# Forty scratch writes issued by GpSimd's queue instead of SyncE's, in a kernel of local attention and a long convolution

## The chip, the cores and the metric

The kernel runs on one core of a Trainium2 chip. The core has five engines with instruction queues of their own: TensorE (PE in the profile), VectorE (DVE), ScalarE (ACT), GpSimd (POOL) and SyncE (SP). DMAs are issued by instructions in these queues and carried out by 16 DMA engines that all queues share. The metric is the time of one execution on the device, in microseconds (us). Before the change it is 208.29 us, the median of three runs (208.14, 208.29, 210.05).

## What is computed

Two independent parts, whose results stand side by side in the output (2048 rows, 576 + 576 columns, bf16):

```python
def _A_ref(x, wqkv, wo):            # x: 1 x 2048 x 576
    q, k, v = ...                   # x @ wqkv, 32 heads of 18
    idx = pos[:, None] - off[None, :]            # off = 0, 2, 4, ..., 14
    logits = einsum("bhsd,bhswd->bhsw", q, k[idx]) * scale     # masked where idx < 0
    o = einsum("bhsw,bhswd->bhsd", softmax(logits), v[idx])
    return o @ wo
def _B_ref(q, k, v, shift_k, ssm_k, ssm_D):      # all 2048 x 576
    kv = causal_conv4(k, shift_k) * v            # four taps along the rows
    y = irfft(rfft(kv, 4096) * rfft(ssm_k, 4096))[:2048]       # per column
    return q * (y + kv * ssm_D)
```

Part A is attention over eight earlier rows at a step of two. Part B is a convolution of 2048 rows with a kernel of the same length, in each of 576 columns.

## The kernel before

All inputs fit into SBUF, the on-chip memory, in stages. The order of the work is written out by hand: the string ORDER (lines 18 to 46) lists some 500 steps, and lines 667 to 672 call them one by one. Each engine executes its own instructions in the order in which these calls emit them, and a DMA stands in the queue of the engine that issues it. Waits between engines, and between a DMA and the users of its data, are put in automatically where two instructions touch the same part of a buffer or of a scratch tensor. An engine that waits holds everything behind it in its queue.

Part B multiplies in the frequency domain. A transform of length 4096 (the 2048 rows, padded) is made in two levels. For the first level the rows are taken as 128 x 16; a step transforms two of the 16 columns of rows (`c2` from 0 to 7), for all 576 channels, with one 128 x 128 table each for the real and the imaginary part. There are sixteen such steps: x0 to x7 for the data (`sx`, x_part, line 470) and k0 to k7 for the long kernel (`kp`, k_part, line 479). ORDER has them as x0, x1, x2, x3, k0, k1, x4, x5, k2, x6, x7, k7, k3, k4, k6, k5, with steps of part A between. All of them go through s1_part (line 426): three chunks (`ch` 0 to 2) of 384 columns, each two matmuls (L432) into PSUM and one eviction (L436) by ACT into a staging buffer; L436 calls evac, whose ScalarE instruction is L103 in the profile. After the third chunk the staging buffer is written to scratch in DRAM, Dx or Dk, in two DMAs of 288 KB (L439), one for each half of the channels. Scratch is needed since the second level reads the same numbers with partitions and rows exchanged: in Dx and Dk, 128 partitions each write four rows of 288 elements (576 bytes).

The staging buffers form a ring of two, `vsr` (line 193). So the evictions of a step can begin only when both writes of the step two before have landed.

The second level (k_spec, x_spec, from L541) loads Dk and Dx (L547), evicts spectra by ACT, multiplies them on DVE (g_prod, L563), and transforms back (g_inv, L576). Its results go to scratch Dy by DMAs of 576 KB that GpSimd issues (L581), and are read again for the last level (L637, y_step), multiplied by q and written out.

The long kernel comes with its rows and columns exchanged. It is loaded by 16 transposing DMAs (load_knat, L262) into `kst`, a ring of seven slots, and written out as rows to the scratch tensor Kt in eight DMAs of 288 KB (k_rows, L265, steps `kw`). From Kt, k_tr (L477) loads two columns of rows for each k step. The memory of `kst` is used later for the products of attention (l_mul, L487 and L491).

The convolution of four taps (kv_conv, L455 to L468) runs on DVE ahead of the x steps. Part A is spread over the same time: projections on PE (L377, L384), eight products of q with shifted k on DVE (L487, L491) summed over the head on PE (L504), softmax, products with v (p_mul, L588), sums (L599) and the output projection (L610).

SyncE's queue holds nearly all DMAs: loads, transposes (L262, and L414 and L424 for tables), the writes of L265 and L439, loads from scratch (L477, L547, L637) and the writes of the output. GpSimd's queue holds a few memsets and index patterns at the start, then one memset (L389, which clears the left edge of V), three small DMAs that copy edge columns of V between partitions (v_halo, L393, 96 partitions x 6 x 16 elements), and the eight Dy writes.

Of the kernel before, what the change touches and what calls it, by code (L numbers as in the profile page):

```python
# [49 lines left out]
def kernel(  # L50
# [13 lines left out]
    nc = tc.nc  # L64
# [33 lines left out]
    def psb():  # L98
        return psum("b", 2, 512)

    def evac(dst, src, scale=None, on="s"):
        if (how["ev"] or on) == "s":
            nc.scalar.activation(dst, src, ACT.Copy, **({} if scale is None else {"scale": scale}))  # L103
        elif scale is None:
            nc.vector.tensor_copy(dst, src)
        else:
            nc.vector.tensor_scalar(dst, src, scale, None, op0=ALU.mult)

    Kt = dram.tile([S, D], BF16, name="Kt")
# [5 lines left out]
    def by_f1(Dd, dh, r0, n):  # L115
        return Dd[dh].rearrange("r f d -> f r d")[:, r0:r0 + n, :]
# [82 lines left out]
    kst = Ring(*[r2.take(2, D) for _ in range(7)])  # L199
# [62 lines left out]
        nc.sync.dma_start_transpose(st[:, b % 2:b % 2 + 1, :], B_ssm_k[:, 128 * b:128 * b + 128])  # L262

    def k_rows(g):
        nc.sync.dma_start(Kt[256 * g:256 * g + 256, :].rearrange("(b p) d -> p b d", p=128), kst[g])  # L265
        kst.drop(g)

    def load_D():
# [157 lines left out]
    def s1_part(src, key, c2, ch, Dd, add_d):  # L426
        sf = src.rearrange("p t d -> p (t d)")
        vst = vsr.get((key, c2)) if ch == 0 else vsr[(key, c2)]
        ps = psb()
        for ri in range(2):  # L430
            extra = add_d and c2 == 0 and ri == 0 and ch < 2
            nc.tensor.matmul(ps[:, ri, 0:384], T1[:, ri, :], sf[:, 384 * ch:384 * ch + 384], start=True, stop=not extra)  # L432
            if extra:
                n = 384 if ch == 0 else 192
                nc.tensor.matmul(ps[:, ri, 0:n], row0[0:1, :], Db[0:1, 384 * ch:384 * ch + n], start=False, stop=True)
        evac(vst[:, :, 384 * ch:384 * ch + 384], ps[:, :, 0:384])  # L436
        if ch == 2:
            for dh, (d0, d1) in enumerate(DCH):
                nc.sync.dma_start(by_f1(Dd, dh, 4 * c2, 4), vst.rearrange("p r (t d) -> p (r t) d", t=2)[:, :, d0:d1])  # L439
            vsr.drop((key, c2))  # L440

    def wqt_step():
# [27 lines left out]
    def x_part(c2, ch):  # L470
        c = c2 // 2
        s1_part(tAr[c][:, 2 * (c2 % 2):2 * (c2 % 2) + 2, :], "x", c2, ch, Dx, False)
        if c2 % 2 and ch == 2:
            tAr.drop(c)
# [4 lines left out]
    def k_part(c2, ch):  # L479
        s1_part(ktr[c2], "k", c2, ch, Dk, True)  # L480
        if ch == 2:
            ktr.drop(c2)
# [160 lines left out]
    def y_step(i, u):  # L643
# [11 lines left out]
        if u:  # L655
# [4 lines left out]

    STEP = dict(tj=t_junk, wm=warm, t0=t_ident, t1=t_pad, tv=t_padv, t2=t_first, t3=t_second, tw=t_w2, t4=t_heads, t5=t_mask,
                lwq=load_wq, wt=wqt_step, lx=load_x, xt=x_tr, ia=ia_table, im=ia_minus, ib=ib_table, kw=k_rows, lwt=load_wqt, ld=load_D, sk=sk_step, qk=qk_step, qt=qk_tail_step, lk=load_k, lv=load_v, lwv=load_wv,
                lkn=load_knat, lwo=load_wo, cv=kv_conv, sx=x_part, kt=k_tr, kp=k_part, v=v_step, vz=v_zero, vh=v_halo, lm=l_mul, lb=l_sum,
                sm=softmax, kl=lambda i: w_load(Dk, "k", i), xl=lambda i: w_load(Dx, "x", i),
# [38 lines left out]
```

## Time and profile before

| | us |
|---|---|
| median of three runs | 208.29 |
| the profiled execution, as timed | 211.04 |
| its span, first to last instruction | 209.1 |
| PE busy | 185.2 |
| DVE busy | 177.8 |
| ACT busy | 160.7 |
| POOL busy | 12.9 |

The profile is of one execution. Busy times count instructions that compute; a DMA is seen by its issue on an engine's queue (SPq is SyncE's queue, POOL GpSimd's), by its landing, and by its packets. q1 in the profile is the DMA queue that SyncE feeds, q0 the one that GpSimd feeds. The granted TensorE clock was 0.999 of full speed. From the list of DMA issues (number, size of one, median us from issue to landing):

| transfer | issued by | number | KB | us to landing |
|---|---|---|---|---|
| Dx written | SP | 16 | 288 | 4.2 |
| Dk written | SP | 16 | 288 | 4.4 |
| Kt written | SP | 8 | 288 | 3.6 |
| Dx loaded | SP | 8 | 576 | 5.9 |
| Dk loaded | SP | 8 | 576 | 6.8 |
| Dy written | POOL | 8 | 576 | 6.2 |
| V's edge columns | POOL | 3 | 18 | 7.6 |

The Kt writes are issued from 34.0 to 51.4 us, the Dx writes from 41.6 to 86.2 and the Dk writes from 62.8 to 106.3.

### The profile page before, as it was taken

The numbers are of one execution on the slowest core, as the hardware profiler recorded it, in microseconds if no ns is written. First come the engines' busy times: TensorE is split into PE (matmuls) and PEld (weight loads), VectorE is DVE, ScalarE is ACT, GpSimd is POOL, SyncE is SP. The second block draws the span as 40 slices with busy tenths as digits, with TensorE's granted clock in tenths as the row PEclk, the third lists the DMA queues.
The fourth block names the chain that finished last, engine by engine and source line by source line (L and its number), as shares of the span: only waits on it lengthen the run. The fifth ranks groups of instructions, "written<-read, shape, count | busy, mean of one in ns | idle before, by whom it ended". The sixth has DMA issues, their size and how long they took to land.

```text
span 209.1 us, 6223 instructions
## 1 busy us (share of the span) xinstructions
PE 185.2 (89%) x2645; PEld 118.3 (57%) x2645; DVE 177.8 (85%) x157; ACT 160.7 (77%) x244; POOL 12.9 (6%) x39
## 2 busy tenths in 40 slices
PE   0899999999989797999789888799999999989890
PEld 0655454444435564554367665566766778766680
DVE  6529999999899999899798989989999979954452
ACT  3669876989777896989799999899999982515421
POOL 8300000000000000001000201110102011000000
PEclk9999999999999999999999999999999999999999
DMA  5999999999997979899997998999799599899894
GB/s 162 317 316 396 239 211 158 311 198 299 275 368 247 260 181 261 241 214 367 261 250 226 264 242 240 310 350 246 256 390 246 179 330 377 248 335 304 223 314 135
DMA packets 66797, 56.20 MB, mean 269 GB/s; under 512 B 16673, under 2 KB 60306, under 8 KB 66770
## 3 DMA queue, kind: packets, MB, share of 16 engines
q1 hardware_dynamic: 65520, 51.04, 91.9%
q0 software_dynamic: 1248, 4.77, 5.9%
q8 instruction: 20, 0.33, 0.7%
q14 instruction: 7, 0.06, 0.1%
q10 hardware_dynamic: 2, 0.00, 0.0%
HBM read 31.04 MB, written 21.23 MB: 250 GB/s over the span
## 4 chain that ended last, share of the span: by engine, by line
PE 46%; ACT 27%; DMA 16%; issue 6%; DVE 2%; SPq 0%; ACTq 0%; DVEq 0%
ACT area L103 24%; PE psB L377 8%; PE psA L377 5%; DMA Dx<-area 5%; PE psA L610 5%; DMA out_dram<-area 4%; DMA Dy<-area 4%; PE psA L384 3%; PE psA L576 3%; PE psB L599 3%; PE psB L432 2%; DMA Dk<-area 2%; PE psA L599 2%; PE psA L432 2%; DMA area<-in_B_shift_k_dram 2%
## 5 line engine op out<-in xcount | busy, mean ns | idle before, releaser
L103 ACT ACTIVATE area<-psA 128x576 bf16<-128x576 f32 (+7 forms) x117 | 83.5, 757 | 33.1 <-PE psB L610 15.0
L103 ACT ACTIVATE area<-psB 128x576 bf16<-128x576 f32 (+5 forms) x113 | 80.2, 757 | 7.9 <-PE psB L377 4.0
L588 DVE TENSOR_TENSOR area<-area,area 128x4096 bf16<-128x4096 bf16 x18 | 40.6, 2284 | 0.9 <-DMA area<-area 0.8
L487 DVE TENSOR_TENSOR area<-area 128x4096 bf16<-128x4096 bf16 x16 | 35.8, 2286 | 1.0 <-PE psA L504 0.7
L377 PEld LDWEIGHTS <-area 128*128 128x128 bf16 x160 | 15.5, 98 | 17.5
L377 PE MATMUL psB<-area,area 128*128 128x512 bf16 x100 | 23.1, 379 | 0.0
L563 DVE TENSOR_TENSOR area<-area 128x2304 bf16<-128x2304 bf16 x16 | 21.1, 1351 | 1.3 <-ACT area L103 1.0
L461 DVE TENSOR_TENSOR area<-area,area 128x2304 bf16<-128x2304 bf16 x16 | 21.0, 1348 | 0.0
L541 PEld LDWEIGHTS <-W 128*64 128x64 bf16 x256 | 14.0, 108 | 12.3 <-issue 11.1
L610 PE MATMUL psA<-area,area 32*128 32x288 bf16 x288 | 18.7, 281 | 1.6 <-ACT area L103 1.1
L610 PE MATMUL psB<-area,area 32*128 32x288 bf16 x288 | 18.7, 281 | 0.0
L384 PEld LDWEIGHTS <-area 128*32 128x32 bf16 x360 | 15.2, 142 | 5.6 <-issue 2.8
L599 PEld LDWEIGHTS <-ident 64*64 64x64 bf16 x576 | 15.3, 106 | 5.1 <-issue 3.5
L610 PEld LDWEIGHTS <-area 32*128 32x128 bf16 x576 | 15.5, 93 | 4.6 <-issue 2.2
L384 PE MATMUL psA<-area,area 128*32 128x512 bf16 x280 | 16.7, 384 | 0.4 <-ACT area L103 0.2
L432 PEld LDWEIGHTS <-T 128*128 128x128 bf16 x96 | 8.6, 97 | 14.6 <-issue 9.3
L541 PE MATMUL psB<-area,W 128*64 128x288 bf16 x152 | 14.7, 290 | 1.8 <-ACT area L103 1.1
L455 DVE TENSOR_TENSOR area<-area,area 128x2304 bf16<-128x2304 bf16 x12 | 15.8, 1350 | 0.1
L576 PEld LDWEIGHTS <-IAt 64*128 64x128 bf16 x256 | 12.4, 94 | 5.8 <-issue 1.5
L432 PE MATMUL psB<-area,T 128*128 128x384 bf16 x52 | 12.6, 326 | 3.5 <-ACT area L103 3.5
L377 PE MATMUL psA<-area,area 128*128 128x512 bf16 x60 | 13.9, 379 | 0.0
L576 PE MATMUL psA<-area,IAt 64*128 64x288 bf16 x176 | 13.0, 283 | 0.4
(104 smaller groups left out, 192.0 us busy)
## 6 DMA issues: line engine op xcount, KB each, us to landing
Dx<-area SPq DMA_DIRECT2D x16, 288.0 KB, 4.2
Dk<-area SPq DMA_DIRECT2D x16, 288.0 KB, 4.4
area<-Dx SPq DMA_DIRECT2D x8, 576.0 KB, 5.9
area<-Dk SPq DMA_DIRECT2D x8, 576.0 KB, 6.8
Dy<-area POOLq DMA_DIRECT2D x8, 576.0 KB, 6.2
area<-Dy SPq DMA_DIRECT2D x8, 576.0 KB, 6.2
area<-in_A_wo_dram SPq DMA_DIRECT2D x4, 648.0 KB, 10.2
area<-in_A_x_dram SPq DMA_DIRECT2D x8, 288.0 KB, 5.4
```

The source lines that it names most:

```text
L103: nc.scalar.activation(dst, src, ACT.Copy, **({} if scale is None else {"scale": scale}))
L377: nc.tensor.matmul(ps[:, u, :], w[:, kb, cols[u]:cols[u] + 128], xT[:, j, kb], start=(kb == 0), stop=(kb == 4))
L384: nc.tensor.matmul(ps[32 * a:32 * a + 32, u, :], wv[:, kb, 2 * n + u:D:DH], xT[:, a, kb], start=(kb == 0), stop=(kb == 4), tile_position=( ...
L432: nc.tensor.matmul(ps[:, ri, 0:384], T1[:, ri, :], sf[:, 384 * ch:384 * ch + 384], start=True, stop=not extra)
L461: nc.vector.tensor_tensor(dst, kfull[:, 4 * c + 3 - j:4 * c + 7 - j, :], skb[:, j, :].unsqueeze(1).to_broadcast([128, 4, D]), ALU.mult)
L487: nc.vector.tensor_tensor(prr.get((n, h)), q2[h], k2[h][:, :, o0:o0 + S], ALU.mult)
L541: nc.tensor.matmul(ps[64 * hp:64 * hp + 64, im, 0:HD], W2[:, im, 8 * g + 2 * prl + hp].rearrange("p l f -> p (l f)"), Wt[:, 2 * prl + hp, ...
L563: nc.vector.tensor_tensor(Pv, Xv.unsqueeze(2).to_broadcast([128, 2, 2, 2 * HD]), Kv.unsqueeze(1).to_broadcast([128, 2, 2, 2 * HD]), ALU.mult)
L576: nc.tensor.matmul(ps[:, hp, 0:HD], IAt[r, tab, 4 * g + 2 * hv + u, :], Pp[(i, hv)][r, n, u, :], start=(n == 0), stop=(n == 3), tile_posit ...
L588: nc.vector.tensor_tensor(Pr.get((hv, p)), vv, Lt[:, :, 256 * hv:256 * hv + 256].unsqueeze(2).to_broadcast([128, W, 2, 256]), ALU.mult)
L599: nc.tensor.matmul(ps[64 * b:64 * b + 64, r, 0:256], ident[g, g], P[g, n, :, 128 * b:128 * b + 128], start=(n == 0), stop=(n == W - 1), ti ...
L610: nc.tensor.matmul(pss[e][:, b, 0:HD], Os[hv][g, d // 2, r, 128 * (d % 2):128 * (d % 2) + 128], wo4[g, d, d0:d1], start=(d == 0), stop=(d ...
```

## The change

The eight Kt writes and the 32 writes of first-level results are issued by `nc.gpsimd` in place of `nc.sync`. Their data, shapes and places in the program's order stay as they are.

```diff
     def k_rows(g):
-        nc.sync.dma_start(Kt[256 * g:256 * g + 256, :].rearrange("(b p) d -> p b d", p=128), kst[g])
+        nc.gpsimd.dma_start(Kt[256 * g:256 * g + 256, :].rearrange("(b p) d -> p b d", p=128), kst[g])
         kst.drop(g)
...
         if ch == 2:
             for dh, (d0, d1) in enumerate(DCH):
-                nc.sync.dma_start(by_f1(Dd, dh, 4 * c2, 4), vst.rearrange("p r (t d) -> p (r t) d", t=2)[:, :, d0:d1])
+                nc.gpsimd.dma_start(by_f1(Dd, dh, 4 * c2, 4), vst.rearrange("p r (t d) -> p (r t) d", t=2)[:, :, d0:d1])
             vsr.drop((key, c2))
```

In GpSimd's queue these 40 DMAs stand between the memsets of the start and the first copy of V's edge columns; the memset of L389 comes among them, behind the writes of x5.

## The prediction

> **What bounds the kernel now.** I read the page's first part, the waits of each engine, the chain of waits and the DMA issues, in that order. The page first:
>
> ```profile
> span 209.1 us, 6223 instructions
> PE 185.2 (89%) x2645; PEld 118.3 (57%) x2645; DVE 177.8 (85%) x157; ACT 160.7 (77%) x244; POOL 12.9 (6%) x39
> ...
> q1 hardware_dynamic: 65520, 51.04, 91.9%
> q0 software_dynamic: 1248, 4.77, 5.9%
> ```
>
> No engine alone carries the span, so the stage that changes has to be looked at by itself. It runs from 34 us (first write of the long kernel's rows, Kt) to 110 us (last first-level write, Dk). In windows of 10 us there, from 50 to 110 us, DVE is busy for 9.04, 10.00, 9.13, 8.94, 9.82 and 8.56 us, PE for 9.65, 7.83, 10.00, 8.87, 9.26 and 8.31. So DVE idles 4.5 us in these 60, and PE 6.1: a transfer that came for free could not gain much more than 4 us here. The waits of the same stretch (us in total, times, longest):
>
> ```profile
> ACT area L103 <- DMA Dx<-area: 2.0, 2, 1.6
> ACT area L103 <- PE psB L432: 1.5, 2, 0.9
> ACT area L103 <- DMA Dk<-area: 1.4, 1, 1.4
> ...
> PE psB L432 <- ACT area L103: 3.5, 5, 1.4
> ```
>
> ACT's evictions (L436, through L103) wait for writes of L439 to land, and PE waits in its turn for ACT. The reason is the ring of two staging buffers: the first eviction of a step needs the buffer whose two writes were issued two steps before. The chain of waits shows one turn (start, length, what):
>
> ```profile
> 73.96 0.81 ACT area L103
> 74.77 0.02 issue
> 74.79 0.36 SPq L439
> 75.14 0.04 issue
> 75.19 5.25 DMA Dx<-area
> 80.44 0.02 issue
> 80.46 0.04 ACTq L103
> 80.49 0.04 issue
> 80.54 0.04 ACT area L103
> ```
>
> The eviction ends at 74.77, the pair is issued at 74.79 and 75.19, the second write lands at 80.44, and ACT goes on at 80.54. So it is the latency of a pair of writes, not the issue, that sets the pace. By issues and landings one buffer passes through the steps x1, x3, k1, x5, x6, k7, k4, k5; the links from x3 on start within 0.86, 0.5, 0.1, 0.1, 0.1 and 0.1 us of the landing (61.74 to 62.60; about 70.0 to 70.47; 80.44 to 80.54; 86.56 to 86.66; 95.68 to 95.79; 103.53 to 103.64). That is six links in a row with about 1.8 us of slack in all, and it leads to 105 us, from where ACT is busy for 9.4 to 10.0 of every 10 us until 170: what is lost before is not made good later.
>
> **The change, part by part.** The instruction lists of the two kernels differ only here: 40 DMA issues leave SP's queue and stand in the POOL queue, with the same shapes. So the change does what it says.
>
> *Issue time.* On SP a write costs 0.36 to 0.96 us, about 0.45. POOL's own DMAs last 0.53 us (Dy, 128 rows of 4608 B) and 0.73 to 0.89 (the halo, 576 pieces of 32 B). A first-level write has 512 rows of 576 B, so I take 0.75; a pair is then issued about 0.3 us later than now. SP waits 17.2 us in 13 waits at L439 for ACT; that goes, and loads behind it (L477, L414, L239, L547) leave earlier. This gains nothing by itself: the evictions at the links above wait for landings of writes, and L477's loads are still held by the buffers that PE frees.
>
> *Start and transfer.* The trace's packet records let me follow rows. Of the 16 pairs on SP, the first rows move 0.90 to 3.08 us after the first issue, 1.44 on average, and the last row ends after 4.25 on average. For POOL's queue the same rows are fewer: first packets after 3.63 and 3.37 (halo) and 4.07, 3.08, 1.10, 2.19 and 1.77 us (Dy, where nothing of the queue was in flight), 2.74 on average. The first Dy is issued at 126.72; in the 4 us behind it the DMA view has no line of q0 at all:
>
> ```profile
> DMA packets 411, 1.18 MB, mean 294 GB/s; under 512 B 16, under 2 KB 16, under 8 KB 410
> ## 3 DMA queue, kind: packets, MB, share of 16 engines
> q1 hardware_dynamic: 410, 1.16, 107.0%
> q8 instruction: 1, 0.02, 2.1%
> issues: line engine op xcount, KB each, median us to landing
> Dy<-area POOLq DMA_DIRECT2D x1, 576.0 KB, 7.8
> ```
>
> So a pair starts 2.74 - 1.44 = 1.3 us later. Against that, POOL's packets may be denser: the halo's pieces of 32 B show as one record of 1152 B per DMA engine (51 ns), where SP's writes show 576 B each (29 ns). If rows are packed to 4608 B (178 ns), a pair takes 128 x 178 / 16 = 1.42 us of each DMA engine instead of 1024 x 29 / 16 = 1.86, 0.4 less. Together with the later second issue: 1.3 + 0.3 - 0.4 = 1.2 us a link. The two Dy transfers that had the queue to themselves agree: 6.2 and 5.1 us from issue to last packet, against 4.25 for a pair of the same 576 KB on SP.
>
> *Sum.* Six links of 1.2 us less 1.8 of slack: 7.2 - 1.8 = 5.4 us. Bounds for one link: -0.9 (no start later than 0.9 us, SP's best, and 0.4 of packing) and +3 (below).
>
> *The eight Kt writes.* Five of them stand behind the pair of x1, on POOL as on SP. SP issues them from 47.05 to 51.40 with transposes between; POOL can issue them from about 47.4 in steps of 0.6, the last at about 49.8, and then starts 1.3 us later. So they land about when they do now. DVE's L491 waits 0.9 us for them at 55.36, since its product lies where Kt was staged, and the loads of L477 leave at 55.26: I take 0 here and +-1 us for the range.
>
> *What else stands on POOL.* The memset of L389 (53.1 us now) goes behind x5's pair, to about 76; its columns are first read by products after 111 us. The first halo copy (95.5 us) goes behind k5's pair, to about 107, and its rows are read after 125. The second is issued at 114.96 in any case, as are all Dy writes. All are hidden by that distance; if POOL ran more than 8 us late, the copy that DVE's L588 waits for at 123.24 (0.8 us now) would be late too.
>
> The profiled execution has a span of 209.1 us and took 211.04; the runs' median is 208.29. I add to the median: 208.3 + 5.4 = 213.7 us.
>
> **Rivals.**
>
> *Writes land sooner, and it is faster (0.22).* On SP a pair stands behind earlier loads and transposes: the slowest starts (2.0, 2.0, 2.4, 1.9, 3.1, 1.8 us) all follow such work. A queue of its own could start each at 1.1 us, POOL's best, and pack its rows: 1.1 - 1.44 + 0.3 - 0.4 = -0.4 us a link, and the freed SP serves loads earlier. The visible waits of ACT for writes (3.4 us) would go, and with them most of DVE's 4.5 us: about 204.5. It decides as soon as a pair's latency falls below 4.25 us. Against it, five of seven POOL transfers started after 2 us.
>
> *POOL starts only between DVE's instructions (0.20).* First packets came 0.04, 0.5, 0.7, 0.4 and 0.8 us after the end of a DVE product (halo at 99.11, Dy at 130.79, 143.50, 148.49, 160.85); at 118.33 this fails, 1.8 us after one. L487's products last 2.28 us and fill the stage. Two writes of a pair would each wait, 1.1 us on average and then 2.3: 3 us a link with the later issue, 6 x 3 - 1.8 = 16, so 224. The Trainium skill, in "SBUF — State Buffer", "Who interferes with whom", says that tensor_tensor has no 2-port mode and takes only the read interface, so that descriptor writing by GpSimd should not be held; by that rule this rival has no effect, and these rows do not settle it.
>
> *Latencies are the same, and nothing changes (0.16).* Median landings are alike: 6.2 us for Dy, 5.9 to 6.8 for SP's loads of 576 KB. The best starts are 1.10 and 0.90 us. With 0.2 us a link the slack of 1.8 takes it all: 208.3. The Trainium skill, "DMA: Bandwidth & Descriptors", "Issuing engines are not separate DMA queues", says that issuers share the same 16 DMA engines and that only issue time is saved, and gives first bytes of about 1 and 0.6 us; by these the estimate is 0.4 x 6 - 1.8 = 0.6 us, 208.9. The rows above (2.74 against 1.44) differ from it.
>
> **How the numbers follow.** The forecast (a link 0.5 to 2 us longer) has 0.42 and gives 213.7, with 209.5 to 218.5 as its own range. A measurement here tells about 1% (2.1 us) from no change. Faster by over 1% is the first rival, less its weak end: 0.20. Within 1%: the last rival and the weak ends of forecast and first rival, 0.20. Slower: 0.60. The range leaves out the upper half of the second rival and the best of the first: 205 to 222.
>
> **What would show it.** Right: first packets of pairs 2 us and more after the issue, ACT's waits for Dx and Dk writes of 6 to 10 us instead of 3.4, DVE's idle time from 50 to 110 us of about 10 instead of 4.5, and the stage's last write at about 116 us. Wrong: pairs that end within 4 us of the issue (first rival); DVE products that are longer, or first packets that all follow DVE's ends (second); or a loss that arises ahead of 56 us, at the Kt writes.

## The result, and the profile after

The changed kernel takes 221.62 us, the median of four runs (218.12, 218.97, 224.26, 224.74), beside 209.04 for the kernel before on the same chip: a ratio of 1.0453, with a 95% interval of 1.0344 to 1.0562. A repetition gave 222.87 us (six runs, 219.52 to 228.29) and 1.0603 (1.0424 to 1.0783). Ratios here compare undisturbed executions with undisturbed ones, and so can differ from the ratio of two medians. The loss is thus 9.5 to 13 us by the two ratios, where 5.4 was forecast.

The profiled execution took 224.74 us, at a mean granted clock of 0.950 (before 0.999); the profiled execution of the repetition took 220.50 us at 0.981, and its numbers stand beside the others where they differ. From the first one's page:

```profile
span 223.0 us, 6251 instructions
...
PE 192.0 (86%) x2645; PEld 119.1 (53%) x2645; DVE 178.1 (80%) x157; ACT 161.2 (72%) x244; POOL 42.6 (19%) x79
...
PEclk9999999999959699799958999999999999999998
...
q1 hardware_dynamic: 46448, 39.24, 67.4%
q0 software_dynamic: 4448, 16.57, 24.2%
...
Dx<-area POOLq DMA_DIRECT2D x16, 288.0 KB, 4.4
Dk<-area POOLq DMA_DIRECT2D x16, 288.0 KB, 5.7
```

DVE and ACT do the same work as before, spread over 14 us more. Forty writes came to q0; a packet there has 3.7 KB on the mean (16.57 MB by 4448; all but some small ones have 4608 B), so the rows of 576 B are packed. The median landings, 4.4 and 5.7 us, are hardly above those of before (4.2 and 4.4), and they count from a write's own issue. What the ring sees is a pair, from its first issue to the landing of both writes (by all completions in the trace): 4.99 us on the mean of the sixteen before, 6.40 after (6.17 in the repetition), and not evenly: 3.9 us for x4, x6 and k6, 12.0 for k3, 8.8 for k4 (9.8 and 6.5 for these two in the repetition).

The waits of each engine (us in total, times, longest) show where the time stands:

```profile
POOL Kt L265 <- DMA area<-in_B_ssm_k_dram: 31.5, 2, 25.7
...
ACT area L103 <- DMA Dk<-area: 7.8, 3, 5.3
DVE area L105 <- PE psA L504: 7.0, 1, 7.0
...
DVE area L487 <- PE psA L504: 6.4, 2, 3.3
...
PE psA L496 <- ACT area L103: 5.3, 1, 5.3
...
PE psA L432 <- DMA area<-Kt: 2.9, 1, 2.9
```

ACT waits for first-level writes, PE waits for ACT, DVE waits for PE. POOL's own wait of 25.7 us costs nothing: before the first pair it waits for ACT once more. The chain of waits holds the worst turn (start, length, what):

```profile
101.96 0.43 POOL Dk L439
102.39 0.31 issue
102.70 11.25 DMA Dk<-area
113.95 0.02 issue
113.98 0.04 ACTq L103
114.01 0.04 issue
114.06 0.82 ACT area L103
114.88 0.04 issue
114.92 0.60 PE psA L496 x2
115.52 1.76 PE psA L504 x9
117.28 0.02 issue
117.30 0.70 DVE area L105
```

k3's second write needs 11.25 us to land; then ACT, PE and DVE go on one behind the other within 3.4 us. DVE's busy time between 50 and 110 us, summed from the windows, is 47.5 us (in both profiles of the changed kernel): 12.5 idle, where before it was 4.5.

Why k3's pair is so late is seen in SyncE's queue. Its timeline before, around k3 and k4 (start, length, what; the pairs are L439):

```profile
93.35 0.91 SPq L439 DMA_DIRECT2D Dk<-area  x2
94.36 0.50 SPq L477 DMA_DIRECT2D area<-Kt  x1
94.95 0.78 SPq L547 DMA_DIRECT2D area<-Dx  x1
98.03 0.93 SPq L439 DMA_DIRECT2D Dk<-area  x2
```

and after, just ahead of k3's pair, which GpSimd issues at 101.96:

```profile
100.13 0.31 SPq L477 DMA_DIRECT2D area<-Kt  x1
100.64 0.86 SPq L547 DMA_DIRECT2D area<-Dx  x2
101.54 4.24 SPq L414 DMA_TRANSPOSE IAt<-W  x2
```

The order of the program is the same. But before, a pair that waited for ACT's eviction held SyncE's queue, and the loads behind it came after it. Now nothing holds them: three loads that stood behind k3's pair (288, 576 and 576 KB: the 1440 KB that the packet records show outstanding when the pair is issued) and a transpose are issued ahead of it; the last load and the transpose stood even behind k4's pair. In the DMA view of 103.6 to 106.2 us, with both writes of the pair issued, the only queue that moves anything is SyncE's:

```profile
DMA packets 186, 0.77 MB, mean 298 GB/s; under 512 B 17, under 2 KB 17, under 8 KB 186
## 3 DMA queue, kind: packets, MB, share of 16 engines
q1 hardware_dynamic: 186, 0.77, 89.2%
```

The pair's first packet moves 4.31 us after its issue. When nothing is in flight it is otherwise: k6's pair is issued at 116.6, and in the view of 116 to 118 us (40 slices of 0.05 us) the DMA engines stand still until 117.9:

```profile
DMA  0000000000000000000000000000000000000299
...
q0 software_dynamic: 13, 0.06, 8.6%
...
Dk<-area POOLq DMA_DIRECT2D x2, 288.0 KB, 3.0
```

The first packet comes 1.33 us after the issue, and the pair has landed after 3.9.

### The profile page after: what moved, and what is told of

Read it like the earlier page. It is cut to its first block, busy times and chain, and to the rows that moved or that the text cites. A ratio compares the mean times of both kernels' runs of the same rounds, so it can differ in the third digit from the quotient of the medians.

```text
span 223.0 us, 6251 instructions
## 1 busy us (share of the span) xinstructions
PE 192.0 (86%) x2645; PEld 119.1 (53%) x2645; DVE 178.1 (80%) x157; ACT 161.2 (72%) x244; POOL 42.6 (19%) x79
## 3 DMA queue, kind: packets, MB, share of 16 engines
q0 software_dynamic: 4448, 16.57, 24.2%
## 4 chain that ended last, share of the span: by engine, by line
PE 34%; DMA 31%; ACT 14%; issue 11%; DVE 5%; SPq 2%; POOL 1%; ACTq 0%; POOLq 0%; DVEq 0%
ACT area L103 13%; DMA Dk<-area 8%; DMA area<-in_B_ssm_k_dram 6%; PE psA L610 5%; DMA Kt<-area 4%; DMA Dy<-area 3%; DMA IAt<-W 3%; PE psB L377 3%; PE psA L576 3%; PE psB L599 3%; PE psA L384 3%; DMA area<-Kt 2%; DMA out_dram<-area 2%; PE psA L504 2%; PE psA L599 2%
## 5 line engine op out<-in xcount | busy, mean ns | idle before, releaser
L103 ACT ACTIVATE area<-psA 128x576 bf16<-128x576 f32 (+7 forms) x117 | 83.5, 756 | 46.2 <-PE psB L610 14.9
L487 DVE TENSOR_TENSOR area<-area 128x4096 bf16<-128x4096 bf16 x16 | 35.9, 2287 | 7.9 <-PE psA L504 6.4
L432 PEld LDWEIGHTS <-T 128*128 128x128 bf16 x96 | 9.3, 105 | 20.4 <-issue 16.0
L541 PEld LDWEIGHTS <-W 128*64 128x64 bf16 x256 | 13.9, 109 | 10.9 <-issue 9.6
L384 PE MATMUL psA<-area,area 128*32 128x512 bf16 x280 | 18.7, 419 | 0.4 <-ACT area L103 0.2
L439 POOL DMA_DIRECT2D Dk<-area x16 | 11.9, 751 | 29.4 <-ACT area L103 25.5
L432 PE MATMUL psB<-area,T 128*128 128x384 bf16 x52 | 14.0, 362 | 3.4 <-ACT area L103 3.4
L439 POOL DMA_DIRECT2D Dx<-area x16 | 12.0, 752 | 23.2 <-ACT area L103 23.2
L576 PEld LDWEIGHTS <-IAt 64*128 64x128 bf16 x256 | 12.5, 94 | 5.8 <-issue 1.8
## 6 DMA issues: line engine op xcount, KB each, us to landing
area<-in_A_wo_dram SPq DMA_DIRECT2D x4, 648.0 KB, 10.3
```

Source lines behind the costliest of these rows:

```text
L384: nc.tensor.matmul(ps[32 * a:32 * a + 32, u, :], wv[:, kb, 2 * n + u:D:DH], xT[:, a, kb], start=(kb == 0), stop=(kb == 4), tile_position=( ...
L439: nc.gpsimd.dma_start(by_f1(Dd, dh, 4 * c2, 4), vst.rearrange("p r (t d) -> p (r t) d", t=2)[:, :, d0:d1])
L487: nc.vector.tensor_tensor(prr.get((n, h)), q2[h], k2[h][:, :, o0:o0 + S], ALU.mult)
L541: nc.tensor.matmul(ps[64 * hp:64 * hp + 64, im, 0:HD], W2[:, im, 8 * g + 2 * prl + hp].rearrange("p l f -> p (l f)"), Wt[:, 2 * prl + hp, ...
```

## Experiments

The times, with the mean pair and DVE's busy time between 50 and 110 us of the profiled execution (before: 4.99 and 55.5; the changed kernel: 6.40 and 47.5, in the repetition 6.17 and 47.5). "-": the executions lie too far apart for an interval.

| kernel | median us (runs; range) | ratio to before | pair us | DVE us |
|---|---|---|---|---|
| Kt writes alone on GpSimd | 210.08 (10; 208.71 to 211.27) | 1.0038 (0.9996 to 1.0081) | 5.05 | 54.6 |
| first-level writes alone on GpSimd | 220.66 (4; 217.84 to 222.26) | 1.0534 (1.0452 to 1.0617) | 6.19 | 47.8 |
| changed, tables copied plainly | 217.31 (4; 216.57 to 218.17) | 1.0351 (1.0286 to 1.0416) | 6.20 | 48.4 |
| before, tables copied plainly | 209.17 (10; 207.68 to 210.6) | 0.9989 (0.9947 to 1.0031) | 4.76 | 53.6 |
| first-level writes on ACT's queue | 233.99 (4; 227.94 to 235.99) | - | 5.25 | 46.2 |
| changed, SyncE held | 218.89 (4; 213.33 to 219.47) | - | 6.10 | 50.1 |
| changed, SyncE held, tables plain | 216.13 (6; 214.19 to 218.48) | 1.0352 (1.0231 to 1.0474) | 5.64 | 52.6 |
| changed, third buffer | 214.5 (4; 210.04 to 215.58) | - | 6.78 | 53.4 |
| before, third buffer | 207.93 (6; 204.57 to 209.8) | 0.9837 (0.973 to 0.9945) | 5.17 | 57.9 |
| the same again | 206.05 (12; 204.73 to 207.74) | 0.9907 (0.9851 to 0.9963) | 5.30 | 57.9 |
| changed, all three | 210.99 (12; 207.24 to 213.93) | 0.9982 (0.9934 to 1.003) | 5.71 | 57.3 |
| changed, no transposing DMA | 214.43 (6; 213.03 to 217.8) | 1.0261 (1.0218 to 1.0304) | 5.71 | 49.8 |
| before, no transposing DMA | 208.28 (12; 206.56 to 210.73) | 0.9977 (0.9941 to 1.0014) | 4.64 | 55.9 |

### Which of the two edits

The change in its two halves, each alone:

```diff
-        nc.sync.dma_start(Kt[256 * g:256 * g + 256, :].rearrange("(b p) d -> p b d", p=128), kst[g])
+        nc.gpsimd.dma_start(Kt[256 * g:256 * g + 256, :].rearrange("(b p) d -> p b d", p=128), kst[g])
```

> Only the eight Kt writes are issued by GpSimd; the Dx and Dk writes stay on SyncE. Theory 1 (GpSimd's writes and SyncE's transposing DMAs slow one another while both are in flight): the first Kt writes run beside the long kernel's transposes as in the changed kernel and the last transposes land near 50 us again, but IAt's transposes find no writes of GpSimd beside them; a loss of 1 to 4 us on 208.5, at the first Kt loads. Theory 2 (a write on GpSimd's queue always starts 1.3 us later): 0 to 1.3 us. Theory 3 (GpSimd's order: a Kt write that waits for a transpose holds the x writes behind it): no x writes stand behind it here, so no loss.

```diff
-                nc.sync.dma_start(by_f1(Dd, dh, 4 * c2, 4), vst.rearrange("p r (t d) -> p (r t) d", t=2)[:, :, d0:d1])
+                nc.gpsimd.dma_start(by_f1(Dd, dh, 4 * c2, 4), vst.rearrange("p r (t d) -> p (r t) d", t=2)[:, :, d0:d1])
```

> Only the 32 Dx and Dk writes are issued by GpSimd; the Kt writes stay on SyncE. Theory 1: the slow pairs beside IAt's transposes (k0, k1, x5, k2, k3, k4) are slow again, loss 6 to 11 us on 208.5, and pairs with no transpose beside them land 4 us after the first issue. Theory 2: all pairs about 1.2 us longer than on SyncE, loss about 5 us. Theory 3: no Kt write holds anything on GpSimd, so the loss falls to 3 us or less.

The Kt writes alone: 1.0038, no loss beyond the measurement. The first-level writes alone: 1.0534, the whole of it, with the same picture of pairs (3.9 us for x4, x6 and k6, 9.0 for k3). So it isn't the Kt writes that stand ahead on GpSimd's queue.

### Transposes beside the writes

IAt and IB are made by nine transposing DMAs on SyncE's queue. Here they are plain copies of the same bytes (IAt and IB then hold untransposed tables), in the changed kernel and, as a control, in the kernel before:

```diff
-        nc.sync.dma_start_transpose(IAt[:, zi, 4 * q:4 * q + 4, :], src)
+        nc.sync.dma_start(IAt[:, zi, 4 * q:4 * q + 4, :], src.rearrange("p (h l) -> p h l", l=128))
...
-        nc.sync.dma_start_transpose(IB[:], T1[:].rearrange("p r f -> p (r f)"))
+        nc.sync.dma_start(IB[:], T1[:])
```

> The changed kernel with the nine transposing DMAs of the tables IAt and IB replaced by plain copies of the same bytes (the transposition of these tables is left out). Theory 1: pairs from k0 on land within 4 to 6 us, and 6 to 10 us of the changed kernel's loss goes: about 210 to 213. Theory 2: the pairs stay longer by 1.2 us each and the time stays at 214 or more. Theory 3: the held x writes come before IAt's transposes, so nothing changes: 217 to 224.

> The kernel before with the same nine transposing DMAs replaced by plain copies (the transposition of these tables is left out). Control for the run above. Theory 1: on one queue transposes and writes follow one another, so little is gained: 206.5 to 208.5. If transposes cost the writes as much on one queue, it would be faster than 206.

1.0351 with its control at 0.9989: the table transposes account for one to two points of the loss, not for most of it (217.31 us, where 210 to 213 were expected if they were the cause). k3's pair still takes 9.6 us, with 1832 KB of SyncE's loads issued and not yet moved when it is issued.

A later pair of kernels leaves out the sixteen transposes of the long kernel too, with plain loads in their place (its rows then hold other numbers):

```diff
-        nc.sync.dma_start_transpose(st[:, b % 2:b % 2 + 1, :], B_ssm_k[:, 128 * b:128 * b + 128])
+        nc.sync.dma_start(st[:, b % 2, :], B_ssm_k.rearrange("d s -> (d s)").rearrange("(b p e) -> b p e", p=128, e=D)[b])
```

> The changed kernel without any transposing DMA: the nine of the tables IAt and IB and the sixteen of the long kernel are plain loads and copies of the same bytes (its rows and the tables hold other numbers then). If transposes in flight make GpSimd's transfers long, x0 and x1 fall from 7.4 and 6 us to 4 to 5 us, k0 is issued 2 to 3 us earlier, and the ratio to the control beside it lies at 1.01 to 1.03. If only what SyncE's queue holds outstanding matters, loads included, the pairs from k0 on stay near 6 us and the ratio to the control at 1.03 to 1.04.

> The control: the kernel before without any transposing DMA, writes on SyncE's queue. All theories: 0.985 to 1.0 of the kernel before, pairs in 4.5 to 5 us.

Both mechanisms show. x0 and x1 fall to 4.1 and 4.0 us (7.3 and 6.1 beside the transposes; 3.5 and 3.5 in the control), and k0 is issued at 61.6 us in place of 65.8. From k0 on the pairs stay long (k3 8.9, with 1845 KB outstanding), and ACT still waits for them:

```profile
ACT area L103 <- DMA Dk<-area: 5.4, 4, 2.6
...
ACT area L103 <- DMA Dx<-area: 3.6, 3, 2.0
```

The ratio lies 2.8 points above the control: with no transpose anywhere, about half of the loss is left.

### GpSimd's queue, or any second queue

The 32 first-level writes on ACT's queue, the rest as before:

```diff
-                nc.sync.dma_start(by_f1(Dd, dh, 4 * c2, 4), vst.rearrange("p r (t d) -> p (r t) d", t=2)[:, :, d0:d1])
+                nc.scalar.dma_start(by_f1(Dd, dh, 4 * c2, 4), vst.rearrange("p r (t d) -> p (r t) d", t=2)[:, :, d0:d1])
```

> The kernel before with the 32 Dx and Dk writes issued by ScalarE's queue, right behind their evictions, and the Kt writes on SyncE. It costs ACT's queue 32 x 0.4 to 0.5 = 13 to 16 us of issue, some of it in idle time. If any second queue beside SyncE's does the harm (theories 1 and 4), the pairs land as late as on GpSimd beside transposes and loads, 6 to 8 us, and the time is 218 or more. If it is GpSimd's queue alone, the pairs land in about 5 us as on SyncE and the loss is that of ACT's issue, 3 to 9 us: 211 to 217.

Here too SyncE is not held, and the same three loads (one of Kt, two of Dx) run ahead of k3's pair. The pair is issued at 108.12 and 108.52 us with 1415 KB outstanding. Its first packet moves 4.10 us after the issue, its last ends after 8.5. From 109 to 112.2 us SyncE's queue is again the only one that moves anything (ACT's is q10):

```profile
DMA packets 264, 1.00 MB, mean 313 GB/s; under 512 B 28, under 2 KB 28, under 8 KB 264
## 3 DMA queue, kind: packets, MB, share of 16 engines
q1 hardware_dynamic: 264, 1.00, 98.2%
```

So to be overtaken by loads is not particular to GpSimd's queue. Most pairs are shorter than on GpSimd's: x4, x6, x7 and k6, with nothing outstanding, start after 0.91 us and land after 3.4, and the mean is 5.25 us against 6.40 and 6.17. ACT waits only 2.7 us for Dk and 1.6 for Dx. The outcome fits neither expectation: the mean pair is about as short as on SyncE, but the time is 228 to 236 us. Much of this time is lost elsewhere: the 32 issues take 14.6 us of ACT's own queue, 0.37 to 0.84 us each, between evictions; ACT stands 8.0 us in one wait for a load of the long kernel; and k0's pair is already issued 10.0 us later than in the kernel before, k5's 17.4 us later.

### SyncE held as before

The changed kernel, with a 576-byte write from the staging buffer on SyncE's queue at each pair, so that the loads behind it again wait for the step's last eviction:

```diff
+    mark = dram.tile([16, HD], BF16, name="mark")
...
+            nc.sync.dma_start(mark[(c2 + (8 if key == "k" else 0)):(c2 + (8 if key == "k" else 0)) + 1, :], vst[0:1, 0, 864:1152])
```

> The changed kernel, and in SyncE's queue a write of one row (576 bytes, to a scratch tensor of its own) at the place of each pair, which waits for the same eviction. So SyncE's loads are held as in the kernel before, while the pairs stay on GpSimd. Theory 4 (with SyncE no longer held, loads and transposes run ahead of the pairs, and GpSimd's packets wait for them): the pairs of x5 to k4 fall to 4 to 6 us and 4 to 8 us of the loss goes, 211 to 215. Theory 2 (GpSimd's start is late by itself): 217 or more. Theory 1 (transposes in flight beside the pairs): little changes where IAt's transposes follow a pair at once, 214 to 219.

> The changed kernel, with SyncE's queue held at each step as before by a 576-byte write that waits for the step's last eviction, and with the nine transposing DMAs of the tables IAt and IB as plain copies (the tables hold other numbers then). If the length of a link comes from what SyncE's queue has in flight (loads that ran ahead, and table transposes), both are gone from k0 on: pairs land in 4.3 to 5.3 us, the time falls to 209 to 213 us. If the start of GpSimd's DMAs costs a fixed amount whatever is in flight, pairs stay at 6 us and the time at 216 us or more. The long kernel's own 16 transposes, before 50 us, stay; x0 and x1 stay slow in both cases.

Where the theory says it should, it helps: k3's pair falls from 12.0 us (9.8 in the repetition) to 6.8, with 203 KB outstanding instead of 1440 at its issue, and with plain tables from 9.6 to 8.2. But both times are misses: 218.89 us where 211 to 215 were expected, and 216.13 with plain tables where 209 to 213 were. The first median lies 2.7 us under that of the changed kernel (221.62), with ranges that overlap; with plain tables the hold changes nothing that can be told (1.0352, and 1.0351 without it). So the hold shows what lengthens k3's pair, and not how much of the time that costs. The trace shows one thing that the hold can't give back: SyncE issues the loads behind it within 0.6 us, while GpSimd's second write follows its first after 0.75 and neither moves before 1.33. So a load of 576 KB still gets ahead of part of the pair (k3: writes at 98.28 and 99.03, the load of Dx at 98.85).

### The ring

A third staging buffer from k0 on, in the space of the taps of the convolution, which are no longer used then:

```diff
-    vsr = Ring(r7.take(2, 2 * D), r7.take(2, 2 * D))
+    class Steps(Ring):
+        def get(self, key):
+            i = ["x0", "x1", "x2", "x3", "k0", "k1", "x4", "x5", "k2", "x6", "x7", "k7", "k3", "k4", "k6", "k5"].index(f"{key[0]}{key[1]}")
+            self.own[key] = i % 2 if i < 4 else [2, 0, 1][(i - 4) % 3]
+            return self.slots[self.own[key]]
+    vsr = Steps(r7.take(2, 2 * D), r7.take(2, 2 * D), skb.rearrange("p a d -> p (a d)").rearrange("p (a d) -> p a d", a=2))
```

> The changed kernel with a third staging buffer from step k0 on (the space of the tap weights, free by then), so that a step's evictions wait for the writes of three steps before. If the loss is the latency of the pairs around a ring of two, most of it goes although the pairs stay as slow: 209 to 212. If it is lost elsewhere (Kt rows, loads, TensorE), the time stays above 215.

> The kernel before with the same third staging buffer. ACT's waits for Dx and Dk writes (3.4 us) go; with DVE's idle time of 4.5 us in the stage as the limit, 204.5 to 208.5. If the ring does not bind the kernel before, no change.

In the changed kernel the pairs get no shorter (6.78 us; k3 12.1, k4 10.3, k6 8.3), and still the time falls to 210 to 216 us: late landings cost through the ring. But against the kernel before with the same buffer (207.93 us) 6.6 us remain by the medians, where the change cost 12.6 to 13.3: the third buffer alone takes away about half of the loss, not most of it. What is left of ACT's waits for these writes is one:

```profile
ACT area L103 <- DMA Dk<-area: 3.2, 1, 3.2
```

In the kernel before, the same buffer takes all such waits away and gains 1 to 1.6%. It was run again, since its first interval was wide:

> The kernel before, with a third staging buffer from k0 on, repeated. If the ring of two is what the evictions wait for in the kernel before too, it lies at 0.975 to 0.993 of the kernel before (about 206 to 208 us), and no wait of ACT for the writes of Dx or Dk is left. If the first measurement (0.9837, 0.973 to 0.9945) was chance, it lies at 0.995 to 1.005.

0.9907, with an interval of 0.9851 to 0.9963: this version is faster than both kernels, by about 1% against the kernel before. The page of its profiled execution:

```profile
span 202.9 us, 6222 instructions
...
PE 184.7 (91%) x2645; PEld 118.1 (58%) x2645; DVE 177.5 (87%) x157; ACT 160.5 (79%) x244; POOL 12.9 (6%) x39
```

Last, the changed kernel with the held queue, the plain tables and the third buffer together (the three diffs above):

> The changed kernel with three things at once: the 576-byte write that holds SyncE's queue at each step, plain copies in place of the table transposes (IAt and IB hold other numbers then), and the third staging buffer from k0 on. If the whole loss runs through the ring of two and the first half of the kernel is as quick as before, it lies where the kernel before lies with a third buffer, at 205 to 208 us. If about 3 us of the loss arise ahead of k0, from Kt's writes beside the long kernel's transposes, it lies at 208 to 211 us. If something else on GpSimd's queue costs time, it stays at 212 us or more.

0.9982 by the ratio, the time of the kernel before, with 57.3 us of DVE's work between 50 and 110 us; by the median of all twelve runs (210.99 beside 208.83) it is 1.0% longer. What is left against the kernel before with a third buffer is 0.75 points by the ratios (1.6 us) and 2.7 by the medians. So most of the loss runs through these three things together; the share of each is not told by these runs. The time lies in the band that was expected for a loss ahead of k0 (208 to 211), but k0's pair is issued at 62.9 us, only 0.1 later than in the kernel before.

### The halved clock

In the changed kernel's profile TensorE's clock is granted at half in four stretches, 20.4 us in all (60.7 to 67.5, 74.4 to 77.8, 91.4 to 94.8 and 111.9 to 118.7 us), none in the kernel before until the last microseconds. Over ten executions of it the time follows the clock: 218.12 at 0.981, 228.29 at 0.945, and a straight line through all, carried on beyond the highest clock seen (0.984), gives 215.5 us at 1. To tell a cost from a symptom, TensorE was given matmuls without use where it stood idle:

```diff
+        if (key, c2, ch) == ("k", 0, 0):
+            for _ in range(13):
+                nc.tensor.matmul(ps[:, 0, :], T1[:, 0, :], W2[:, 0, 0:8].rearrange("p h l f -> p (h l f)"), start=True, stop=True)
...
+        for _ in range({("x", 5, 0): 30, ("x", 6, 2): 10, ("x", 7, 0): 14, ("k", 5, 0): 76}.get((key, c2, ch), 0)):
+            nc.tensor.matmul(ps[:, 0, 384:512], T1[:, 0, :], T1[:, 1, :], start=True, stop=True)
```

> The changed kernel once more, as the reference for the three runs beside it. All theories: 217 to 225 us, about 1.04 to 1.06 of the kernel before; pairs of first-level writes land 6 to 6.5 us after the first issue on the mean (4.9 before). If the loss lies partly in the halved TensorE clock, the executions lie apart by the half-clock time they have: those at a mean granted clock of 0.98 near 218 us, those near 0.95 near 224 us.

> The changed kernel, with 143 matmuls more whose results nobody reads, put on TensorE ahead of the four stretches in which it stood idle for 2 to 5 us in the changed kernel's profile (before k0, x5's second chunk, x7, and after k5's first chunk). They take about 12 us of TensorE, meant to lie in its idle time; the pairs of writes stay late. If the halved clock is a cost of its own, the half-clock windows between 50 and 125 us (20.4 us of them in the changed kernel) nearly vanish, and the time falls to 213 to 217 us, 2 us or more under the changed kernel in the same comparison. If the clock is only a symptom (TensorE has slack while it waits for ACT), the time stays at 217 to 224 us with the windows gone. If the added matmuls don't fit into the idle time, it rises instead, to 220 to 230 us.

It went wrong: 239.66 us, 1.15. The matmuls behind an eviction's chunk waited for that eviction, though they write other columns (group: busy and mean, then idle before and its releaser):

```profile
L441 PE MATMUL psB<-T 128*128 128x128 bf16 x116 | 10.1, 269 | 14.2 <-ACT area L103 14.2
```

Only the first 13, ahead of k0, went into idle time, and they were run alone:

> The changed kernel, with 13 matmuls of 512 columns more, whose results nobody reads, in k0's own accumulation bank, ahead of k0's first matmul, where TensorE stood idle for 2.3 to 2.9 us until the long kernel's rows were loaded. Only the first half-clock window (6.8 us from about 60.5 us, in both profiles of the changed kernel) should vanish. If a window costs its lost half, the time falls by up to 3.4 us against the changed kernel (medians 221.6 and 222.9), to about 219. If the windows are a symptom there (the ring of two and ACT hold TensorE anyway), it stays at 220 to 224 us.

The half-clock stretch at 60 us is gone (the first is now at 73.0), and the median is 221.54 us in six runs, where the ten runs of the changed kernel have 222.85: nothing that these runs could tell from no gain. x4's pair is issued at 74.4 us, in the two profiles of the changed kernel at 75.6 and 74.1. So for this stretch no price of the slow clock shows. For the later stretches it stays open. The repetition's profile, without any half-clock stretch between 67.2 and 217.5 us, has the same DVE time between 50 and 110 us as the first (47.45 against 47.50), but issues k5's pair at 114.1 in place of 119.9. It took 220.50 us, 5% more than the kernel before beside it (209.58): a loss of 10 us needs none of the later stretches.

## Why the prediction was right and wrong

- **The place**: right in the main. Late pairs cost through the ring of two (a third buffer takes away about half of the loss while the pairs stay late), not through an engine's busy time or the Kt writes (1.0038 alone), and what is late at k5 stays late: k5's pair is issued 14.0 us later than before (119.9 against 105.9), the span is 13.9 longer (8.2 and 9.6 in the repetition).
- **Issue on POOL, 0.75 us; rows packed to 4608 B**: measured 0.751 to 0.752, and packets of 4608 B. Right.
- **A pair 1.2 us longer**: the mean rose by 1.41 us (4.99 to 6.40; by 1.18 in the repetition). Over the six links that were counted the rises add up to 7.5 us (6.7 in the repetition), where the sum had 7.2. That is luck: one link rose by 0.1 us and another by 3.3 (0.1 and 2.8 in the repetition), and the explanation was wrong. The start after 2.74 us was an average of starts beside other traffic; with nothing in flight a start takes 1.33 us, less than SyncE's average of 1.44 (its best was 0.90). What goes with long starts is what SyncE has outstanding when a pair is issued. Over the profiles of the changed kernel (both), the first-level writes alone, the plain tables, no transposes, and SyncE held with and without plain tables, with the KB issued on SyncE's queue and not yet moved worked out from packet records, the first packet comes after 1.65 us on the mean (under 50 KB, 61 pairs), 2.68 (50 to 300 KB, 27), 2.75 (300 to 600 KB, 15) and 4.32 (over 600 KB, 9; none under 3.03). Single starts scatter widely about the first three means (1.32 to 3.65 us under 50 KB, up to 5.48 between 300 and 600), so the amount outstanding is not all of it.
- **"This gains nothing by itself"**, of SP freed of its 13 waits at L439: this is the step that failed. It was asked only what earlier loads could gain, not what they would be put ahead of. Those waits kept loads and transposes behind the pairs. With them gone, k3's pair rose by 7.1 us (4.9 to 12.0; to 9.8 in the repetition, to 9.0 with the first-level writes alone), where the sum had 1.2 for any link; and k3 isn't among the six links counted at all, as it goes through the other buffer. There it holds k6's step: k4's pair is issued 9.3 us later than before, k6's 13.8 (6.9 and 8.6 in the repetition). That loads run ahead and that k3's pair is long with them shows on GpSimd's queue and on ACT's, and the pair shortens when SyncE is held. How many microseconds of the whole this step is worth stays open.
- **"I take 0 here and +-1 us"** for what lies ahead of 56 us: the Kt writes alone cost nothing, but k0's pair is issued 3.0 and 2.1 us later in the two profiles of the changed kernel. The first load of Kt lands there 5.3 and 5.7 us after its issue, 3.4 before. With the first-level writes alone on GpSimd it takes 5.1 us too, but leaves at 54.3 us (56.1 and 54.8 in the changed kernel), and k0 is only 0.2 us late. So this term belonged into the sum; in the times (1.0534 beside 1.0453 and 1.0603) it can't be told.
- **Writes land sooner** (first rival): only where SyncE has nothing in flight, and not even there: 3.9 us for x4 and x6, 3.6 and 3.8 before; k6 gained (4.7 to 3.9).
- **POOL starts only between DVE's instructions** (second rival): refuted. In the profiles of the eleven kernels that have all first-level writes on GpSimd's queue, 52 pairs moved their first packet 1.30 to 1.36 us after the issue, and 26 of these within a DVE instruction, 0.2 us or more from either end. L487 takes 2287 ns as before. The Trainium skill, "SBUF — State Buffer", "Who interferes with whom", says that tensor_tensor takes only the read interface of the shared ports and leaves descriptor writing free (inferred there); this agrees with it.
- **No change** (third rival): refuted by the interval. "Issuing engines are not separate DMA queues" in the Trainium skill's "DMA: Bandwidth & Descriptors" says that DMAs of all issuers interleave on the same engines. Between 103.6 and 106.2 us the trace shows no such interleaving: 186 packets of SyncE's queue, none of GpSimd's, which had both writes issued. As ACT's queue shows the same (109 to 112.2 us above), it is not something of GpSimd's queue alone; why the engines did not interleave no run here tells.
- **Two readings** of the prediction are off, without weight in the sum: a write on SyncE took up to 1.60 us to issue (not 0.96), and the shorter of the two Dy transfers ended its last packet after 4.9 us (not 5.1).
- **What would show it**: ACT's waits for the writes of 6 to 10 us (7.8 for Dk), DVE's idle time of about 10 us (12.5), the last write at about 116 us (its first half issued at 119.9, in the repetition at 114.1).

How the 9.5 to 13 us divide between overtaking loads, transposes and clock is not settled as a sum: the causes lengthen the same links, and one taken away leaves the next.

## What to carry to other kernels

A queue that waits also orders: before DMAs are moved off it, list what stands behind each wait, and ask where those transfers go once nothing holds them. Here three loads went ahead of a pair that they had stood behind, and it waited over 4 us for its first packet, on either of the two queues tried. A latency that feeds a ring of buffers is counted turn by turn and for each buffer, with what is in flight at that turn, since one turn of 12 us costs more than its share of a mean. Where a ring of two waits for landings, a third buffer in memory that has become free was worth more here (about 1%) than either other queue that was tried.

## What the hardware showed unexpectedly

- With nothing else in flight, and nothing issued on SyncE's queue meanwhile, GpSimd's first packet came 1.32 to 1.34 us after the issue, ACT's after 0.91. With over 600 KB outstanding on SyncE's queue it was 3.0 to 5.1 us on GpSimd's, and 4.10 in the one such case on ACT's.
- Transposing DMAs lengthen the writes of GpSimd's queue beside them, and are longer themselves. Without any transpose x0 and x1 take 4.1 and 4.0 us in place of 7.3 and 6.1. The last seven transposes of the long kernel, which run beside these pairs and the Kt writes, land after 4.3 to 7.0 us, where it was 3.2 to 5.3 before. The two transposes of IAt beside k3's pair land after 12.4 and 11.4 us (in the kernel before it was 2.5 to 5.8 up to 110 us), but they stand behind 1440 KB of loads too.
- Half-clock stretches last 3.4 or 6.8 us. Three of the four in the changed kernel's profile begin in or shortly behind an idle time of TensorE of over 2 us: idle from 71.9 to 74.0, half clock from 74.4. The Trainium skill, "TensorE: Matmul & The Clock Gate", "What's actually happening", gives a window of about 3.4 us and a drop after an idle one; the lengths agree with it, but a gap of 2.1 us was enough here. The length of a single gap does not decide: ahead of the stretch from 91.4 us no gap is over 0.92, and in the repetition a gap of 2.4 us (107.3 to 109.7) is followed by none.
